# Attention, gated layer and softplus layer on one core: where 1/rms is applied for the first 1024 tokens of layer 1

## The chip, the core and the metric

The kernel runs on one core of one Trainium2 chip. The metric is the device time of one execution in microseconds; the time before is the median of three runs. All times below come from those runs and from one profiled execution.

## What is computed

```python
# q, k, v: (4, 8, 576, 64); x: 2304 tokens x 512
scores = scale * np.matmul(q, k.transpose(0, 1, 3, 2))
scores = np.where(masks[None], scores, -1e9)        # 4 heads local, 4 heads strided
attn = softmax(scores)                              # + 1e-9 in the divisor
x = np.matmul(attn, v) -> (2304, 512)

rms = np.sqrt(np.mean(x * x, axis=-1, keepdims=True) + 1e-06)
xn = x / rms * rms_g
g = xn @ w_gate                                     # 512 x 1536
silu = g * (1.0 / (1.0 + np.exp(-g)))
y = silu * (xn @ w_val) @ w_out                     # 1536 x 512

h = y @ w_in                                        # 512 x 2048
out = (np.maximum(h, 0.0) + np.log1p(np.exp(-np.abs(h)))) @ w_out2
```

Attention over 4 batches of 576 tokens with 8 heads gives x, 2304 tokens of 512 features. Layer 1 divides each token by its root mean square, multiplies by a gain for each feature, and forms silu(gate) * value through 1536 hidden features. Layer 2 is a softplus layer through 2048 hidden features. The division by rms is one number for each token, so it commutes with the products over features: a gate or a value made of undivided x is the true one times rms.

## The kernel before, in words

**Layout.** Features lie on the 128 partitions, tokens along the free dimension. x (the tile xs) is four blocks of 128 features (kk = 0 to 3). The tokens are cut into chunks of 512 (CUTS): chunks 0 and 1 are side A (tokens 0 to 1023), chunks 2, 3 and 4 (256 tokens) side B. The hidden features of layer 1 are 12 blocks of 128, called f in the code and hidden blocks here.

**Products.** Each fp32 operand is split in two rounded parts: ScalarE copies it to the rounded type (L351 for x, L405 and L425 for weights) and VectorE or GpSimd subtracts (L355 on VectorE, L356 on GpSimd). A product is three matmuls (mm3, L434): high by high, high by low, low by high. On side A each gate or value of a chunk is 12 matmuls into one bank (plain). On side B, and in layer 2, a product of 2 x 2 blocks is done with seven instead of eight block products (quad), from sums of chunks that combine builds and sums of weights.

**Attention and its place.** The first 16 of 32 attention units (two batches) run by themselves, with the weights of hidden blocks 0 and 1 decoded beside them. Chunk 0 is complete before these units end: at step 12 the function early works out its statistics, normalizes it, splits it and starts its first gate and value. The other 16 units are dealt out beside hidden blocks 0 to 9 of side A.

**Statistics.** stats (L440) squares the four blocks of x on ScalarE (L452), sums them over partitions and blocks with matmuls by a matrix of -1/512 (L453), takes logarithm and exponential on ScalarE (L457, L458), does one correction step in three VectorE instructions (L459, L461, L462) and leaves 1/rms in the tile ssq. norm (L467) then scales x in place: one fused VectorE instruction for each of the four blocks (L472), which multiplies by the gain and by 1/rms.

```python
def early():                       # L999, chunk 0; chunk 1 has the same three steps at L1071
    use.s = s_banks
    stats(0, f_banks)
    direct(0)                      # split_op of the four blocks of x
    half(0, 0, f_banks)            # gate and value of hidden block 0
```

**Gate chain.** chain1 (L860) reads a gate out of its bank with SiLU on ScalarE (L867) into a work tile of the ring gv, multiplies by the value out of its bank on VectorE (L868), and splits the result (L856 and L355) for the output product. out1 (L885) adds output products into x's own place (L899 for the first, L901 for all others).

**Work tiles.** The ring gv has two tiles of its own. Once chunks 0 and 1 are normalized, their 1/rms is of no more use, and the two halves of ssq join the ring (L1078), which then has four. From then on gates, statistics, the temporaries of combine and the copies of quad (L816) take turns on the four.

**Order.** The instructions are first noted in Program, each with an engine, a duration estimate and what it reads and writes. emit (L89) plays them through a model of the engines (Trial), eight times with due times that follow from the last play, and issues the best play's order, which then stands for every engine, queues of SyncE and GpSimd included. Two programs are emitted: up to hidden block 9 of side A with all of attention, and all that follows. An element-wise instruction added with two (L354) may be put on VectorE or on GpSimd.

Of the kernel before, what the change touches and what calls it, by code (L numbers as in the profile page):

```python
# [10 lines left out]
F32 = mybir.dt.float32  # L11
# [17 lines left out]
CH = 512  # L29
# [7 lines left out]
W1N, W2N = DFF // 128, DF2 // 128  # L37
DEALT = 10
LT, LT2, LV, EB = 4, 4, 5, 5
WARM = 9  # L40
# [207 lines left out]
def attn_glu_softplus(  # L248
# [99 lines left out]
    def split_op(src, ksrc, slot, k, n0=0, eng="POOL"):  # L348
# [3 lines left out]
        sub(eng, n, l, src, h.bitcast(F32), [ksrc, kh], [kl])  # L352

    def two(eng, n, name, o, x, y, r, w):  # L354
        pr.add("DVE", 68 + n / 0.96, lambda: getattr(nc.vector, name)(o, x, y), r, w,  # L355
               alt=(110 + n * 2.3, lambda: getattr(nc.gpsimd, name)(o, x, y)))  # L356
# [3 lines left out]

    hold = []

    def decode(src, t, kt, keep):

        raw, kraw = raws.next()
        u, ku = cvu.next()
        words = raw.bitcast(U32).rearrange("p (n two) -> p n two", two=2)
        wlo, whi = words[:, :, 0], words[:, :, 1]
        dma(512, lambda: nc.sync.dma_start(out=raw, in_=src), hold, [kraw])
        act(512, lambda: nc.scalar.activation(t, whi.bitcast(F32), AF.Copy, scale=2.0 ** -112), [kraw], [kt])  # L370
        dve(512, lambda: nc.vector.tensor_scalar(out=u, in0=t.bitcast(U32), scalar1=0x80000000, scalar2=None,
                                                 op0=ALU.bitwise_and), [kt], [ku], True)
        dve(512, lambda: nc.vector.scalar_tensor_tensor(  # L373
            out=u, in0=wlo, scalar=29, in1=u, op0=ALU.logical_shift_right, op1=ALU.bitwise_or),
            [kraw, ku], [ku])
        dve(512, lambda: nc.vector.scalar_tensor_tensor(
            out=t.bitcast(U32), in0=t.bitcast(U32), scalar=3, in1=u,
            op0=ALU.logical_shift_left, op1=ALU.bitwise_or), [kt, ku], [kt])
        dma(256, lambda: nc.sync.dma_start(out=wk[keep], in_=t), [kt], [("wk", keep, keep + 1)])

# [59 lines left out]
    def stats(c, ring_):  # L440
# [5 lines left out]
        for i, kk in enumerate((0, 2, 1, 3) if c < 2 else (0,)):  # L446
            y, ky = r, kr
            if c < 2:
# [14 lines left out]
                                                       op0=ALU.add, op1=ALU.mult), [kr, ks], [kr])  # L463
        if c < 2:
            norm(c, "DVE")
# [12 lines left out]
    def attention(at, use):  # L478
# [5 lines left out]
        mask = at.tile([128, MW], BF16, name="mask")  # L484
        dma(100, lambda: nc.sync.dma_start(out=mask, in_=masks), [], [all_of("mask")])
        vb = ring(at, "vb", 2, [128, 9, 128])
        eb = ring(at, "eb", EB, [128, 5 * LK])
        pp = ring(at, "pp", 2, [128, 6, 128])
        pt = ring(at, "pt", 4, [128, 3 * 128])
        sq = ring(at, "sq", 2, [128, 6 * SK])  # L490
        mz = ring(at, "mz", 8, [128, 2, 6])
# [29 lines left out]
        def load_v(u):  # L521
            b, p, t0, n = units[u]
            kp, nt = (LK, 9) if p < 2 else (128, 6)
            vt, (kv, _, _) = vb.next()
            src = vl[b, p] if p < 2 else vs[b, p - 2]
            vals[u // 2] = (vt, kv)
            dma(nt * (48 if p < 2 else 50), lambda: nc.sync.dma_start(out=vt[:kp, :nt, :], in_=src), [], [all_of(kv)])

# [118 lines left out]
        def stage_v(u):  # L647
# [8 lines left out]
            for a in range(n):  # L656
                t, kt = pts[a // 3]
                for h in range(2):
                    o = (2 * (a % 3) + (h ^ (u % 2))) * nq
                    pr.add("PE", 59, lambda a=a, h=h, o=o, t=t: nc.tensor.matmul(  # L660
                        xb[64 * h:64 * h + 64, a * nq:(a + 1) * nq], lhsT=vt[r0:r1, v0 + a, 64 * h:64 * h + 64],
                        rhs=t[r0:r1, o:o + nq], start=True, stop=True), [all_of(kv), kt],
                        [kx], mode=1 if loc else 3)
# [195 lines left out]

    def chain1(gate, val, n=CH, r4=False, eng="POOL"):  # L860
        (gb, kg), (vb_, kv) = gate, val
        if "bank" in kg[0]:
            a, ka = fk["gv"].next()
        else:
            a, ka = gb, kg
        a, gb, vb_ = a[:, :n], gb[:, :n], vb_[:, :n]
        act(n, lambda: nc.scalar.activation(a, gb, AF.Silu), [kg], [ka], True)  # L867
        dve(n, lambda: nc.vector.tensor_mul(a, vb_, a), [kv, ka], [ka])  # L868
        return halves(a, ka, n, eng, r4)
# [108 lines left out]
    with tc.manual_schedule():  # L978
# [9 lines left out]
        def direct(c):  # L988
            slots = (B11, B21) if c % 2 == 0 else (B12, B22)
            for kk in range(KD):  # L990
                x, kx = xview(kk, CUTS[c], CUTS[c + 1])
                split_op(x, kx, slots[kk // 2], kk % 2, eng="DVE" if kk % 2 or c and kk < 3 else "POOL")

        gates = {}

        def half(f, c, ring_):
            gates[f, c] = [plain(w_at(f, 0), row, c, ring_) for row in (0, 1)]

        def early():  # L999
            use.s = s_banks  # L1000
            stats(0, f_banks)
            direct(0)
            half(0, 0, f_banks)

        def prepare(f, parts, u):
# [13 lines left out]

        dma(64, lambda: nc.sync.dma_start(out=id_sb, in_=ident), [], [all_of("id")])  # L1020
        dma(2, lambda: nc.sync.dma_start(out=rg_sb, in_=rg), [], [all_of("rg")])
# [13 lines left out]
        def side_a(f, queue):  # L1035

            if f > 1 and f != DEALT:
                prep1(f, 0)
            w = w_at(f, 0)
            for c in (0, 1) if f > 1 else (1,):  # L1040
                gate, val = gates.pop((f, c), (None, None))
                gate = gate or plain(w, 0, c, f_banks)
                step(queue)
                drain(1)
                val = val or plain(w, 1, c, f_banks)
                step(queue)
                g[f, c] = chain1(gate, val, eng="DVE" if f < DEALT else "POOL")
                drain(1 if f < W1N - 1 else 0)
                step(queue)
            if f % 2:  # L1050
                todo.extend(outs1(f, f == 1, (0, 1) if f > 1 else (1,)))

        with ExitStack() as c2:
# [7 lines left out]
            for f in (0, 1):  # L1061
                g[f, 0] = chain1(*gates.pop((f, 0)))
            o_banks.t = f_banks.t
# [5 lines left out]
            o_banks.keys = {}  # L1069
            table(EXP_LN)  # L1070
            stats(1, t_banks)  # L1071
            table("silu_and_others")
            direct(1)
            half(0, 1, v_banks)
            tv = Ring(banks.t[2:4], "bank", 2)
            use.t = use.v = tv
            for i in (0, 1):
                fk["gv"].keys[len(fk["gv"].t)] = ("ssq", i * CH, i * CH + CH)  # L1078
                fk["gv"].t.append(ssq[:, i * CH:i * CH + CH])
# [5 lines left out]
            prep1(DEALT, 0)  # L1085
            pr.emit()
        o_banks.t = banks.t[4:6] + banks.t[2:4]
        o_banks.keys = {i: (f"bank{i}", 0, 1 << 20) for i in (2, 3)}
# [5 lines left out]
        for f in range(DEALT, W1N):  # L1094
            side_a(f, [None, None, (last_turn,)] if f == DEALT else [])
            if f == DEALT:
                combine(*SIDES[1][:2], False)
        drain(len(todo))
        o_banks.t, o_banks.keys = banks.t[4:], {}
        build(*SIDES[1], False)  # L1100
# [117 lines left out]
```

## Time and profile before

| | us |
|---|---|
| median of 3 runs | 901.63 |
| lowest, highest | 901.39, 902.55 |
| profiled execution | 900.52 |
| its span, first to last instruction | 898.7 |
| TensorE busy | 882.7 |
| VectorE busy | 712.9 |
| ScalarE busy | 486.1 |
| GpSimd busy | 28.1 |

PE is TensorE's matmul, PEld its weight load, DVE VectorE, ACT ScalarE, POOL GpSimd, SP SyncE. The span lies 1.8 us below its execution's time. Busy time of one engine says nothing by itself of who waits; for that there are the idle times with what ended them, and the chain of work that ended last. A line such as L355 is a helper's and serves many tiles, so groups are told apart by tiles: "ob<-xs,ob" writes the low part of x's operand, "win<-w,win" that of a weight.

### The profile page before, as it was taken

To read this page: it belongs to the slowest core of one execution; us is meant where nothing else is said; L and a number is where in the kernel's file an instruction comes from. 1 tells how busy PE (TensorE), PEld (TensorE's weight loads), DVE (VectorE), ACT (ScalarE), POOL (GpSimd) and SP (SyncE) were. 2 spreads that over 40 slices of the span, in tenths; PEclk is the share of its full clock that TensorE was granted. 3 is DMA by queue.
4 is the path that set the end of the run, shared out by engine and by line. 5 is a ranking of instruction groups with operands and counts; after the bars stand their busy time and mean duration, and the time that the engine had idled before them with its cause. 6 is when DMAs were issued, how large, how long until landed. Compare 5 with 4: busy or idle time off the path is not lost.

```text
span 898.7 us, 14075 instructions
## 1 busy us (share of the span) xinstructions
PE 882.7 (98%) x5320; PEld 725.7 (81%) x5320; DVE 712.9 (79%) x1349; ACT 486.1 (54%) x999; POOL 28.1 (3%) x26
## 2 busy tenths in 40 slices
PE   7899999999999999999999999999999999999998
PEld 6567777778777888888888888888888888888886
DVE  4988898998599995888988799877798456676644
ACT  5987664545364675444545567544474655434331
POOL 0000010200000000000100100000000000000000
PEclk7999999999999999999999999999999999999999
DMA  7874667363040443344553025321114111111003
GB/s 254 263 228 146 205 205 224 124 214 106 13 141 23 151 152 105 134 146 140 183 154 104 2 85 178 137 71 48 47 47 153 36 47 48 47 32 39 1 1 117
DMA packets 41858, 102.18 MB, mean 114 GB/s; under 512 B 4800, under 2 KB 5568, under 8 KB 41792
## 3 DMA queue, kind: packets, MB, share of 16 engines
q1 hardware_dynamic: 41792, 101.31, 35.5%
q8 instruction: 41, 0.67, 0.3%
q14 instruction: 25, 0.20, 0.1%
HBM read 78.74 MB, written 22.54 MB: 113 GB/s over the span
## 4 chain that ended last, share of the span: by engine, by line
PE 67%; DVE 3%; issue 0%
PE bank L434 67%; DVE xs L901 1%; DVE ob L355 0%; DVE tb L355 0%; DVE xs L355 0%; DVE win L355 0%; DVE w L355 0%; DVE ssq L355 0%; DVE glx L355 0%; DVE xs L919 0%; DVE gv L355 0%; DVE ssq L868 0%; DVE gv L868 0%; DVE gl L355 0%
## 5 line engine op out<-in xcount | busy, mean ns | idle before, releaser
L434 PE MATMUL bank<-ob,win 128*128 128x512 f32 (+1 forms) x1560 | 430.8, 360 | 2.7 <-ACT ob L351 1.8
L434 PEld LDWEIGHTS bank<-ob,win 128*128 128x128 f32 x1560 | 283.4, 188 | 55.0 <-ACT ob L351 2.2
L434 PE MATMUL bank<-tb,win 128*128 128x512 f32 x672 | 232.8, 392 | 0.0
L434 PEld LDWEIGHTS bank<-tb,win 128*128 128x128 f32 x672 | 125.4, 188 | 22.9 <-DVE xs L901 0.4
L919 DVE TENSOR_TENSOR xs<-bank,xs 128x512 f32<-128x512 f32 x126 | 86.8, 689 | 45.7 <-PE bank L434 44.4
L405 ACT ACTIVATE win<-w 128x512 fp32r<-128x512 f32 (+1 forms) x136 | 83.4, 616 | 63.9 <-PE bank L434 32.7
L355 DVE TENSOR_TENSOR win<-w,win 128x512 fp32r<-128x512 f32 (+1 forms) x134 | 89.5, 673 | 15.6 <-ACT win L405 12.6
L434 PE MATMUL bank<-wout,ghx 128*128 128x512 f32 x304 | 100.0, 390 | 0.0
L434 PE MATMUL bank<-wout,gh 128*128 128x512 f32 x272 | 90.4, 390 | 0.0
L434 PE MATMUL bank<-ghx,wout 128*128 128x512 f32 x224 | 84.1, 394 | 0.0
L434 PE MATMUL bank<-gh,wout 128*128 128x512 f32 (+1 forms) x256 | 81.3, 356 | 0.5 <-DVE xs L901 0.4
L901 DVE TENSOR_TENSOR xs<-bank,xs 128x512 f32<-128x512 f32 (+1 forms) x100 | 62.2, 628 | 8.9 <-PE bank L434 8.1
L434 PEld LDWEIGHTS bank<-wout,ghx 128*128 128x128 f32 x304 | 56.9, 188 | 11.7
L434 PEld LDWEIGHTS bank<-wout,gh 128*128 128x128 f32 x272 | 50.9, 188 | 10.6
L816 ACT ACTIVATE gv<-bank 128x512 f32<-128x512 f32 x48 | 28.4, 592 | 48.1 <-PE bank L434 47.6
L434 PE MATMUL bank<-wout,glx 128*128 128x512 f32 x152 | 53.2, 389 | 0.0
L434 PEld LDWEIGHTS bank<-gh,wout 128*128 128x128 f32 x256 | 45.5, 189 | 9.0 <-DVE xs L901 1.4
L434 PEld LDWEIGHTS bank<-ghx,wout 128*128 128x128 f32 x224 | 41.9, 188 | 8.4 <-ACT ghx L856 0.2
L434 PE MATMUL bank<-wout,gl 128*128 128x512 f32 x136 | 47.7, 389 | 0.0
L373 DVE SCALAR_TENSOR_TENSOR cvu<-raw,cvu 128x512 uint32<-128x512 uint32 x68 | 46.6, 686 | 1.0
L355 DVE TENSOR_TENSOR w<-w 128x256 f32<-128x256 f32 x109 | 45.4, 416 | 0.9
L820 DVE TENSOR_TENSOR gv<-bank,gv 128x512 f32<-128x512 f32 x48 | 32.9, 685 | 16.0 <-ACT gv L816 9.0
(131 smaller groups left out, 1211.8 us busy)
## 6 DMA issues: line engine op xcount, KB each, us to landing
raw<-w SPq DMA_DIRECT2D x68, 512.0 KB, 4.1
w<-w_kept SPq DMA_DIRECT2D x56, 256.0 KB, 2.6
w_kept<-cvtx SPq DMA_DIRECT2D x26, 256.0 KB, 3.7
cvt<-w_kept SPq DMA_DIRECT2D x26, 256.0 KB, 2.7
w_kept<-w SPq DMA_DIRECT2D x24, 256.0 KB, 4.2
qk<-qk SPq DMA_DIRECT2D x8, 601.0 KB, 5.6
w_kept<-cvt SPq DMA_DIRECT2D x18, 256.0 KB, 3.5
cvtx<-w_kept SPq DMA_DIRECT2D x18, 256.0 KB, 2.8
```

Source lines behind the costliest of these rows:

```text
L355: pr.add("DVE", 68 + n / 0.96, lambda: getattr(nc.vector, name)(o, x, y), r, w, alt=(110 + n * 2.3, lambda: getattr(nc.gpsimd, name)(o, x, ...
L373: dve(512, lambda: nc.vector.scalar_tensor_tensor(out=u, in0=wlo, scalar=29, in1=u, op0=ALU.logical_shift_right, op1=ALU.bitwise_or), [kra ...
L405: act(n, lambda: nc.scalar.activation(h, t, AF.Copy), [kt], [reg(0, o + lo, o + hi)])
L434: lambda a=a, b=b, i=i, st=st, mv=mv: nc.tensor.matmul(o, lhsT=st[a], rhs=mv[b], start=(first and i == 0), stop=(last and i == m - 1), ski ...
L816: act(CH, lambda: nc.scalar.activation(o, y[0], AF.Copy), [y[1]], [ko])
L820: dve(CH, lambda: nc.vector.tensor_add(o[0], y[0], o[0]), [y[1], o[1]], [o[1]])
L901: dve(n, lambda: nc.vector.tensor_add(x, pb, x), [kp, kx], [kx])
L919: dve(DM, lambda: nc.vector.tensor_add(x, pb, x), [kp, kx], [kx])
```

## The change

For chunks 0 and 1 x is not divided by rms ahead of layer 1. The operands are split from x times the gain alone (raw_op): a ScalarE copy with the gain as scale, and a fused VectorE instruction that multiplies and subtracts. The first gates and values of a chunk are noted ahead of its statistics. chain1 multiplies the gate by 1/rms on VectorE, out of the bank into the work tile, ahead of SiLU, which then works in place; the value stays undivided, and x is multiplied by 1/rms once after the last output product of side A (eight instructions that may go to VectorE or GpSimd). As ssq is needed until then, the ring gv gets two other tiles (gvx) while attention lives, goes back to two when the first program has been emitted, and gets the halves of ssq after the final multiplies. Some duration estimates in the planner change too: loads of weights, masks, values and of the identity (64 to 40), and the value products of the strided heads.

```diff
+RAW = (0, 1)
...
+    def raw_op(src, ksrc, slot, k, kk):
+        (h, l), (kh, kl) = op_of(slot, k)
+        g, kg = rg_sb[:, kk:kk + 1], all_of("rg")
+        act(CH, lambda: nc.scalar.activation(h, src, AF.Copy, scale=g), [ksrc, kg], [kh])
+        pr.add("DVE", 130 + CH / 0.96, lambda: nc.vector.scalar_tensor_tensor(
+            out=l, in0=src, scalar=g, in1=h.bitcast(F32), op0=ALU.mult, op1=ALU.subtract), [ksrc, kh, kg], [kl])
...
-        dma(512, lambda: nc.sync.dma_start(out=raw, in_=src), hold, [kraw])
+        dma(340, lambda: nc.sync.dma_start(out=raw, in_=src), hold, [kraw])
...
-        dma(256, lambda: nc.sync.dma_start(out=wk[keep], in_=t), [kt], [("wk", keep, keep + 1)])
+        dma(170, lambda: nc.sync.dma_start(out=wk[keep], in_=t), [kt], [("wk", keep, keep + 1)])
...
-        if c < 2:
+        if c < 2 and c not in RAW:
             norm(c, "DVE")
...
-        dma(100, lambda: nc.sync.dma_start(out=mask, in_=masks), [], [all_of("mask")])
+        dma(140, lambda: nc.sync.dma_start(out=mask, in_=masks), [], [all_of("mask")])
...
+        gvx.update((i, at.tile([128, CH], F32, name=f"gvx{i}")) for i in RAW)
...
-            dma(nt * (48 if p < 2 else 50), lambda: nc.sync.dma_start(out=vt[:kp, :nt, :], in_=src), [], [all_of(kv)])
+            dma(nt * (31 if p < 2 else 41), lambda: nc.sync.dma_start(out=vt[:kp, :nt, :], in_=src), [], [all_of(kv)])
...
-                    pr.add("PE", 59, lambda a=a, h=h, o=o, t=t: nc.tensor.matmul(
+                    pr.add("PE", 59 if loc else 36, lambda a=a, h=h, o=o, t=t: nc.tensor.matmul(
...
-    def chain1(gate, val, n=CH, r4=False, eng="POOL"):
+    def chain1(gate, val, n=CH, r4=False, eng="POOL", c=None):
...
+        if c in RAW:
+            r, kr = sview(CUTS[c], CUTS[c + 1]), ("ssq", CUTS[c], CUTS[c + 1])
+            dve(n, lambda a=a, gb=gb: nc.vector.tensor_mul(a, gb, r), [kg, kr], [ka])
+            gb, kg = a, ka
         act(n, lambda: nc.scalar.activation(a, gb, AF.Silu), [kg], [ka], True)
...
         def direct(c):
...
+                if c in RAW:
+                    raw_op(x, kx, slots[kk // 2], kk % 2, kk)
+                    continue
                 split_op(x, kx, slots[kk // 2], kk % 2, eng="DVE" if kk % 2 or c and kk < 3 else "POOL")
...
+        def give(cs):
+            for c in cs:
+                fk["gv"].keys[len(fk["gv"].t)] = ("ssq", c * CH, c * CH + CH)
+                fk["gv"].t.append(ssq[:, c * CH:c * CH + CH])
...
         def early():
             use.s = s_banks
-            stats(0, f_banks)
             direct(0)
             half(0, 0, f_banks)
+            stats(0, v_banks)
...
             table(EXP_LN)
+            direct(1)
+            half(0, 1, v_banks)
             stats(1, t_banks)
             table("silu_and_others")
-            direct(1)
-            half(0, 1, v_banks)
...
             for i in (0, 1):
+                if i in RAW:
+                    fk["gv"].keys[len(fk["gv"].t)] = (f"gvx{i}", 0, CH)
+                    fk["gv"].t.append(gvx[i])
+                    continue
                 fk["gv"].keys[len(fk["gv"].t)] = ("ssq", i * CH, i * CH + CH)
...
             pr.emit()
+            if RAW:
+                fk["gv"].t, fk["gv"].keys = fk["gv"].t[:2], {}
+                give(i for i in (0, 1) if i not in RAW)
...
         drain(len(todo))
+        for c in RAW:
+            for kk in range(KD):
+                x, kx = xv(kk, c)
+                two("POOL", CH, "tensor_mul", x, x, sview(CUTS[c], CUTS[c + 1]), [kx, ("ssq", CUTS[c], CUTS[c + 1])], [kx])
+        give(RAW)
```

## Rows read from the trace of the kernel before

**Rows 1.** The page: busy time, share and instructions of each engine.

```profile
PE 882.7 (98%) x5320; PEld 725.7 (81%) x5320; DVE 712.9 (79%) x1349; ACT 486.1 (54%) x999; POOL 28.1 (3%) x26
```

**Rows 2.** Windows: length, then busy us (x instructions) of PE, PEld, DVE, ACT, POOL; clock, DMA.

```profile
28.00:77.00 49.00, 42.95 (x478) 29.16 (x474) 41.91 (x100) 44.15 (x144) 0.00 (x0) 1.00 0.68 215
77.00:244.00 167.00, 166.60 (x1303) 131.89 (x1302) 144.15 (x292) 89.05 (x159) 13.35 (x10) 1.00 0.51 159
244.00:264.00 20.00, 19.98 (x87) 15.90 (x86) 19.47 (x33) 14.19 (x22) 1.41 (x1) 1.00 0.50 147
264.00:291.00 27.00, 26.25 (x114) 20.67 (x112) 27.00 (x49) 14.06 (x26) 1.29 (x1) 1.00 0.10 28
291.00:320.00 29.00, 29.00 (x153) 24.60 (x152) 28.12 (x56) 18.22 (x33) 1.30 (x1) 1.00 0.42 137
```

**Rows 3.** The chain that ended last: start us, us, what.

```profile
289.46 0.61 DVE xs L901
...
291.31 223.95 PE bank L434 x1172
```

**Rows 4.** TensorE's waits over the span: us in total, times, longest.

```profile
PE bank L434 <- ACT ob L351: 1.8, 2, 1.4
...
PE bank L453 <- ACT gv L452: 1.0, 2, 0.5
...
PE bank L637 <- DVE pp L355: 1.0, 1, 1.0
...
PE bank L434 <- DVE xs L901: 0.6, 2, 0.4
```

**Rows 5.** TensorE in order of time: start us, us, what, [idle before].

```profile
44.40 0.73 PE L434 MATMUL bank<-ob,win 128*128 128x512 f32 x2 [1.36 <-ACT ob L351]
...
76.55 8.02 PE L434 MATMUL bank<-ob,win 128*128 128x512 f32 x34 [0.39 <-ACT ob L351]
```

**Rows 6.** VectorE in order of time, the same columns.

```profile
42.72 2.07 DVE L472 SCALAR_TENSOR_TENSOR xs<-xs,rg_sb,ssq 128x512 f32<-128x512 f32 x3
...
257.32 2.38 DVE L355 TENSOR_TENSOR xs<-xs,ssq_b 128x512 f32<-128x512 f32 x2
...
278.30 0.68 DVE L355 TENSOR_TENSOR gv<-xs,ssq 128x512 f32<-128x512 f32 x1
...
279.83 0.67 DVE L355 TENSOR_TENSOR win<-w,win 128x512 fp32r<-128x512 f32 x1
...
280.43 0.68 DVE L901 TENSOR_TENSOR xs<-bank,xs 128x512 f32<-128x512 f32 x1
...
286.84 0.68 DVE L355 TENSOR_TENSOR tb<-gv,tb 128x512 fp32r<-128x512 f32 x1
...
289.38 1.87 DVE L901 TENSOR_TENSOR xs<-bank,xs 128x512 f32<-128x512 f32 x3
...
298.23 0.69 DVE L373 SCALAR_TENSOR_TENSOR cvu<-raw,cvu 128x512 uint32<-128x512 uint32 x1
```

**Rows 7.** Groups by line and shape: busy us, mean ns, idle before.

```profile
L472 DVE SCALAR_TENSOR_TENSOR xs<-xs,rg_sb,ssq 128x512 f32<-128x512 f32 x8 | 5.6, 745 | 0.0
...
L867 ACT ACTIVATE gv<-bank 128x512 f32<-128x512 f32 x13 | 7.8, 599 | 7.7 <-PE bank L434 6.4 <-DVE tb L355 1.2
...
L867 ACT ACTIVATE gv<-gv 128x512 f32<-128x512 f32 x12 | 7.6, 633 | 10.2 <-DVE gv L820 10.1
```

**Rows 8.** ScalarE in order of time.

```profile
58.58 0.28 ACT L281 ACTIVATE xs<-bank 128x128 f32<-128x128 f32 x1
...
58.91 0.37 ACT L281 ACTIVATE xs<-bank,rg_sb 128x128 f32<-128x128 f32 x1
...
276.13 0.58 ACT L867 ACTIVATE ssq<-bank 128x512 f32<-128x512 f32 x1
...
295.05 0.60 ACT L816 ACTIVATE gv<-bank 128x512 f32<-128x512 f32 x1 [4.48 <-PE bank L434]
```

**Rows 9.** GpSimd in order of time.

```profile
257.14 1.41 POOL L356 TENSOR_TENSOR xs<-xs,ssq_b 128x512 f32<-128x512 f32 x1 [48.80 <-DVE ssq_b L462]
```

## What the change is expected to do

> **What bounds the kernel now.** I read the page first: TensorE is busy 98% of the span, VectorE 79% [rows 1]. An average says little here, so next come windows cut where the work changes [rows 2]. TensorE is idle 6.05 us between 28 and 77 us (49.00 - 42.95), 0.4 us between 77 and 244, 0.75 between 264 and 291, and nothing from 291 to 320. From 77 us on TensorE is the bound, and what the change can win lies almost wholly ahead of 77. VectorE is the close second: full between 264 and 291 (27.00 of 27.00), nearly full from 244 to 320, but with 22.85 us to spare between 77 and 244. The chain that ended last says the same: it runs through VectorE up to 290 us, then through matmuls without a break [rows 3].
>
> TensorE's own waits [rows 4] tell what ends its idle time. Two kinds belong to this change: 1.8 us for the rounded operand of x (the copy of L351) and 1.0 us for squares (L452), in sum 2.8 us. TensorE's order of time says where [rows 5]: the first layer-1 products of chunk 0 start at 44.40 after 1.36 us of idleness, those of chunk 1 at 76.55 after 0.39. In between TensorE is not starved: scores, value products and the output products of the first two hidden blocks fill it.
>
> **Part by part.** One 512-wide VectorE instruction costs its engine 0.60 us: the addition out of a bank at 280.43 follows the subtraction at 279.83 by that much, and of three additions in 1.87 us the last is 0.68 long [rows 6]. The fused scaling of L472 costs 0.66: three in 2.07 [rows 6], one being 0.745 long [rows 7].
>
> [...]
>
> *Removed:* eight scalings of x (L472), 8 x 0.66 = 5.3 us of VectorE, four from 42.72 on, four around 76. With them goes the wait of the first products for the whole statistics chain: squares, sums, logarithm, exponential, three VectorE steps, scalings.
>
> *Added to the operands:* the copies of L351 get a per-partition scale, and the eight subtractions become fused ones at 0.66: 8 x 0.06 = 0.5 us more of VectorE, which the 5.3 us pay. The scaled copy has no row at this size; nothing at one end, 0.09 us each at the other, after the 128-wide pair at 58.58 and 58.91, 0.28 without and 0.37 with the scale [rows 8]. I take 0.09, 0.7 us in all; between 28 and 77 ScalarE has 4.85 us to spare [rows 2], and without that cover the 0.7 us would come on top.
>
> *Moved:* squares, sums and root of both chunks go behind the first gate and value products and use other banks; TensorE's work stays the same, so only idle time can be won. The 2.8 us of rows 4 go, since the rounded copies now need x alone; what is late next are chunk 0's weights (L405, L355). The other 3.25 us between 28 and 77 end on attention's exponentials, on weights and on probabilities such as those of L637 [rows 4]. They may stay (0) or go whole (3.25): on ScalarE four squares and two root steps no longer precede exponentials and weights, while four scaled copies do. No row is nearer to one end, so I take half, 1.6. The front gives **4.4 us**, with bounds 0 and 6.05.
>
> *Gate multiplies:* 24 at 0.60. Two (chunk 0, blocks 0 and 1) lie near 60 us, 18 between 77 and 244: 10.8 us into 22.85 us of slack. I cost them at nothing; without the cover TensorE would pay at most 10.8. They lengthen each chain by one step; a bank is wanted again only after a group of 12 matmuls, more than 2 us later, so this hides too. SiLU now reads SBUF, 633 against 599 ns [rows 7], nothing on an engine that is busy 89.05 of 167 us. The last four (blocks 10 and 11) fall between 244 and 291, where VectorE has 0.53 us left: 4 x 0.60 - 0.53 = **1.9 us**, charged in full, because TensorE there already waits for VectorE's additions [rows 3, 4].
>
> *Final multiplies:* eight, 4.8 us on VectorE or more on GpSimd, after the last additions of chunks 0 and 1 (three in 1.87 us from 289.38 on [rows 6]) and ahead of the next use of the two halves of ssq as work tiles. After 291 VectorE also decodes layer-2 weights (298.23 [rows 6]), which nothing needs soon and which can give way: I take 0 and keep 4.8 as the other end.
>
> *Work tiles:* from block 10 to the end of side A two instead of four serve the gate chains, the statistics and six temporaries of the sums for chunks 2 and 3. No row shows it. One end is 0. The other: the last gate chain took a tile at 276.13 [rows 8], and with two it would wait for the last temporary, written at 278.30 and read until 286.84 + 0.68 [rows 6], 11.4 us. I take 0: an unhurried temporary needs some 2.5 us (write, copy, subtract, hops), so six through two tiles some 7.5, and TensorE has output products to go on with.
>
> *Planner's estimates:* loads of weights, masks and values and the strided value product get other ones. They cost no time, but reorder every queue, SP's too. I take 0, and 1 us to both sides, the size of the single waits in rows 4.
>
> **Sum.** -4.4 + 1.9 = -2.5 us. The profiled execution took 900.52 (span 898.7 and 1.8 around it), so 898.0; the median of the runs is 1.1 above that execution, so 901.63 - 2.5 = **899.1 us**. About 0.2%, 1.8 us, is what a measurement can tell from no change.
>
> **Rivals.**
> *Nothing measurable (0.27).* The first products start earlier, but TensorE was filled anyway; only the 2.8 us go, and some 2.2 come back from VectorE: 901.0. It also covers a change that doesn't do what it says, because attention's ScalarE work holds x itself up. For it: the 3.25 us end on other things. Against it: ScalarE is relieved where it is nearly full.
>
> *The hand-over pays (0.18).* Between 244 and 300 VectorE has no room, and the ring of work tiles takes back the halves of ssq only after the eight multiplies. Those end at 289.38 + 1.87 + 4.8 = 296.0 if nothing goes between, while the first products of the next chunks were copied into work tiles from 295.05 on [rows 8]. It decides as soon as such a copy lands on a half of ssq before the multiplies are through; behind it a bank stays full and TensorE stands. Price: 12 x 0.60 = 7.2 us, with the front at 2.8: 901.63 + 4.4 = 906.0. For it: TensorE waits for L901 there already. Against it: chunk 0's four can run among chunk 1's additions.
>
> *The shared port (0.05).* While GpSimd multiplied x at 257.14, for 1.41 us [rows 9], VectorE's pair of the same operation took 2.38 us [rows 6] where two steps of 0.60 and 0.68 would have done. If GpSimd takes all eight beside such work, VectorE stands 8 x 1.41 = 11.3 us: 901.63 - 2.5 + 11.3 = 910.4. [...]
>
> *More than the waits (0.06).* All 6.05 us go, and the four multiplies hide: 895.6.
>
> **Numbers.** The forecast (a gain of 1.8 to 5 us) has 0.44. With the larger gain faster is 0.50; same is 0.27; the hand-over and the port make slower 0.23. The range runs from 895.0 (the whole front, with something of the planner's 1 us) to 906.0 (the hand-over); the likeliest case alone covers 896.6 to 899.8.
>
> **What would show it.** Right: the first product of rounded x with weights starts before 40 us, chunk 1's near 71; no L472 rows; TensorE's idle time between 28 and 77 under 3 us; a new VectorE group of 24 multiplies out of a bank; the products of the next chunks start some 2 us ahead of 291. Wrong: idle TensorE behind copies of L816 or behind the final multiplies after 290; a front as idle as now; waits for the multiplied gate in side A.

## The result and the profile after

The changed kernel took 912.38 us (median of four runs, 911.39 to 913.96) against 901.51 on the same chips (899.32 to 902.55): a ratio of 1.0136, interval 1.0113 to 1.016. It is 10.9 us slower; the forecast was 899.1, the range ended at 906.0. The profiled execution has a span of 911.4 us against 898.7.

The page's first part, of after: busy time, share of the span and instructions.

```profile
PE 884.3 (97%) x5320; PEld 727.0 (80%) x5320; DVE 723.6 (79%) x1365; ACT 485.1 (53%) x995; POOL 43.9 (5%) x38
```

Against [rows 1] TensorE's same 5320 matmuls are busy 1.6 us longer and the span is 12.7 longer: the other 11.1 us are TensorE's idle time. Windows of after, columns as in [rows 2], say where most of it lies:

```profile
28.00:77.00 49.00, 42.74 (x470) 31.91 (x468) 43.49 (x103) 39.95 (x134) 7.54 (x6) 0.97 0.72 221
77.00:244.00 167.00, 163.26 (x1216) 126.37 (x1215) 144.52 (x290) 87.94 (x153) 14.11 (x11) 0.99 0.49 152
244.00:264.00 20.00, 18.76 (x132) 14.80 (x133) 17.14 (x31) 14.20 (x23) 0.80 (x1) 1.00 0.45 129
264.00:291.00 27.00, 24.15 (x97) 18.89 (x97) 25.54 (x39) 12.69 (x22) 7.81 (x6) 0.94 0.07 23
291.00:320.00 29.00, 29.00 (x148) 24.61 (x147) 28.87 (x56) 15.18 (x30) 1.62 (x1) 1.00 0.15 46
```

The front, where the gain was to come from, is as idle as before: 6.26 us against 6.05. The stage that had no slack to lose, 77 to 244, is idle 3.74 us against 0.4, and from 244 to 291 4.09 against 0.77. These three make 6.9 us of the 11.1. The rest lies ahead of 28 us, 2.5, and behind 320, 1.8; the first of the two says little, since orders as fast as before (e3 and e8 below) are idle 1.3 and 2.5 us more than before there, too. VectorE's busy share isn't full ahead of 291, but from 258 to 283 us the chain that ended last runs through it with no pause over 1.02 us: there it is the bound.

The chain that ended last, of after (start us, us, what):

```profile
282.38 0.61 DVE gv L878
283.04 55.37 PE bank L442 x269
...
346.84 4.88 DMA w_kept<-cvtx
...
451.45 5.53 DMA w<-w_kept
```

A gate multiply (L878) is now a link of it, the last before 55 us of matmuls. And where [rows 3] show 223.95 us of matmuls without a break, transfers of weights stand in between.

TensorE's waits over the span, of after:

```profile
PE bank L562 <- ACT eb L608: 5.8, 2, 5.1
PE bank L646 <- DVE eb L363: 2.3, 2, 1.4
PE bank L442 <- DVE gv L878: 2.2, 3, 1.3
PE bank L646 <- DVE mz L595: 2.1, 1, 2.1
```

Of [rows 4] the waits for the rounded copies of x and for squares are gone but for 0.3 us (L460, not shown), as forecast. In their place stand attention's own waits and the new multiply's. TensorE in order of time, of after, against [rows 5]:

```profile
33.39 2.68 PE L442 MATMUL bank<-ob,win 128*128 128x512 f32 x10
...
47.99 0.72 PE L646 MATMUL bank<-id_sb,eb 128*96 128x128 f32 x5 [2.13 <-DVE mz L595]
...
50.27 0.30 PE L562 MATMUL bank<-mask 64*64 64x270 bf16 x2 [0.72 <-ACT eb L608]
...
52.52 0.31 PE L646 MATMUL bank<-id_sb,eb 128*96 128x128 f32 x1 [1.37 <-DVE eb L363]
```

Chunk 0's products do start 11 us earlier. Where they stood before, from 44.40 to some 53, attention's exponentials and sums now have nothing beside them, and TensorE stands 4.2 us in three pieces.

The groups by line and shape, of after, answer to [rows 7]; the last two are the fused subtraction and the scaled copy:

```profile
L880 ACT ACTIVATE gv<-gv 128x512 f32<-128x512 f32 x28 | 17.6, 629 | 20.9 <-DVE gv L878 14.9 <-DVE gv L829 5.8
L878 DVE TENSOR_TENSOR gv<-bank,ssq 128x512 f32<-128x512 f32 x16 | 10.9, 685 | 2.0 <-PE bank L442 1.7
L878 DVE TENSOR_TENSOR gvx<-bank,ssq 128x512 f32<-128x512 f32 x8 | 5.5, 685 | 3.2 <-PE bank L442 3.2
L359 DVE SCALAR_TENSOR_TENSOR ob<-xs,rg_sb,ob 128x512 fp32r<-128x512 f32 x8 | 5.9, 749 | 0.0
L358 ACT ACTIVATE ob<-xs,rg_sb 128x512 fp32r<-128x512 f32 x8 | 5.9, 743 | 0.0
```

The L472 rows are gone and 24 multiplies of 0.685 us are there. SiLU used to wait for matmuls, 6.4 us in the group of [rows 7]; now it waits 14.9 us for the multiply.

### The profile page after: what moved, and what is told of

It reads as the page before. It is cut to its first block, busy times and chain, and to the rows that moved or that the text cites. A ratio compares the mean times of both kernels' runs of the same rounds, so it can differ in the third digit from the quotient of the medians.

```text
span 911.4 us, 14103 instructions
## 1 busy us (share of the span) xinstructions
PE 884.3 (97%) x5320; PEld 727.0 (80%) x5320; DVE 723.6 (79%) x1365; ACT 485.1 (53%) x995; POOL 43.9 (5%) x38
## 4 chain that ended last, share of the span: by engine, by line
PE 79%; DVE 9%; DMA 6%; ACT 4%; issue 1%; SPq 0%; ACTq 0%; DVEq 0%
PE bank L442 75%; DMA raw<-w 2%; DMA w_kept<-cvtx 2%; PE bank L669 1%; PE bank L646 1%; DMA qk<-qk 1%; DVE xs L914 1%; PE bank L575 1%; ACT eb L608 1%; DVE cvu L381 1%; DVE win L363 1%; DMA w<-w_kept 1%; DVE gl L363 1%; DVE gv L363 1%; DVE tb L363 1%
## 5 line engine op out<-in xcount | busy, mean ns | idle before, releaser
L442 PE MATMUL bank<-ob,win 128*128 128x512 f32 (+1 forms) x1560 | 439.5, 365 | 3.6 <-DVE gv L878 2.2
L363 DVE TENSOR_TENSOR win<-w,win 128x512 fp32r<-128x512 f32 (+1 forms) x127 | 84.3, 668 | 16.2 <-ACT win L413 13.1
```

Source lines behind the costliest of these rows:

```text
L442: lambda a=a, b=b, i=i, st=st, mv=mv: nc.tensor.matmul(o, lhsT=st[a], rhs=mv[b], start=(first and i == 0), stop=(last and i == m - 1), ski ...
```

## The experiments

The change has two parts that need not go together: x undivided with 1/rms moved behind, and new duration estimates in the planner. I had costed the second at 0 plus or minus 1 us. The theories at the start: the new estimates make a worse order (A); the moved 1/rms costs by itself (B), and there by VectorE's time for the multiplies, by the smaller ring of work tiles, by the final multiplies, or by something else; or any other order of the same instructions gains or loses this much (C). "Before" in each result was measured on the same chip; all times are medians.

**Each part alone.** e1_est_only is before with all six estimates, e2_raw_only the change with the old ones.

```diff
-        dma(512, lambda: nc.sync.dma_start(out=raw, in_=src), hold, [kraw])
+        dma(340, lambda: nc.sync.dma_start(out=raw, in_=src), hold, [kraw])
...
-                    pr.add("PE", 59, lambda a=a, h=h, o=o, t=t: nc.tensor.matmul(
+                    pr.add("PE", 59 if loc else 36, lambda a=a, h=h, o=o, t=t: nc.tensor.matmul(
```

> The kernel before with the change's six duration estimates and nothing else of it. Theory A (the estimates): the planner now believes loads land sooner and issues weight loads ahead of attention's own, so the loss of 11 us is here: 908 to 914 us, TensorE idle some 7 us before 28 us as with the whole change. Theory B (the multiplies and tiles of the moved 1/rms): the estimates alone leave the time within 2 us of before, 899 to 904, whatever the first 28 us look like. Theory C (order luck, any other plan costs or gains some us): anything between 897 and 912, with no part of the loss tied to the loads.

> The whole change with the duration estimates of before. Theory A: the loss goes, 896 to 902 us, and the front gain of some 4 us that the prediction named is seen. Theory B: 909 to 914, with idle TensorE behind the gate multiplies between 77 and 244 us and at the hand-over near 283. Theory C: anything between 897 and 912.

Measured: e1 909.21 (ratio 1.0096, 1.0066 to 1.0126), e2 907.78 (1.0082, 1.0055 to 1.0108). Both cost, 8.5 and 7 us, and together 10.9: they don't add up. e2 lies under the range given for B and far over the one for A.

**How much is the order that happened to be drawn?** emit weighs each play's due times against those of the one before with KEEP = 0.5; another value gives other orders of the same program. e3 is before, e4 the change, both with 0.4; e15 is e1, e16 is e2 with 0.6.

```diff
-TURNS, KEEP, SWITCH, LEAVE = 8, 0.5, 125, 4000
+TURNS, KEEP, SWITCH, LEAVE = 8, 0.4, 125, 4000
```

> The kernel before with one planner constant moved that no instruction knows of (how much of the last play's due times is kept: 0.4 for 0.5). It measures how far another plan for the same instructions moves the time. Theories A and B: within 2 us of before, 899.5 to 903.5. Theory C: off by 4 us or more.

> The changed kernel with the same planner constant at 0.4. Theories A and B: still slower than before by 8 us or more, 909 to 915. Theory C: it falls back by 4 us or more, to 908 or less.

> The six estimates alone, with the planner's constant at 0.6 for another order. If the estimates themselves are the cause (orders made for faster loads and value products lose whatever their detail): 906 to 911 us. If the order found was a poor draw: 904 or less.

> The moved 1/rms with the estimates of before and the constant at 0.6. If the edit is the cause: 905 to 910 us. If a poor draw: 904 or less.

Measured: e3 901.21 (1.0006, 0.9993 to 1.0019), e4 910.25 (1.0115, 1.0081 to 1.0148), e15 905.99 (1.0054, 1.0039 to 1.007), e16 908.8 (1.0073, 1.005 to 1.0096). The loss isn't one unlucky draw, as far as two orders of each can tell. The moved 1/rms costs about the same in both; of the estimates' 8.5 us some 3 are the draw's, and e15 lies between its two forecasts.

**Which estimates?** e7 is before with the two for weights (340 and 170), e8 before with the other four.

> The kernel before with the two estimates for weights alone (loading a weight 340 for 512, keeping it 170 for 256). If the loss of the estimates comes from weight loads put ahead of attention's loads: 905 to 911 us, TensorE idle 7 us or more before 28 us. If it comes from the others: 899 to 903.

> The kernel before with the other four estimates alone (mask, identity, values, strided value product). If weight loads are the cause: 899 to 903 us. If the estimate of the value product or of the values is: 905 to 911.

Measured: e7 903.93 (1.0041, 1.0022 to 1.0061), e8 900.5 (1.0005, 0.9992 to 1.0018). The weights' estimates cost by themselves, less than was said for them; the other four cost nothing alone, and whether they add to the weights' isn't shown: e15, all six in another order, has 1.0054, inside e7's interval. Idle TensorE ahead of 28 us, which was to mark the cause, marks nothing: e8 has 7.4 us of it and is as fast as before.

The chain that ended last of e7 passes through transfers:

```profile
311.63 5.61 DMA w<-w_kept
318.32 0.65 ACT cvtx L370
319.50 70.69 PE bank L434 x374
...
539.36 6.58 DMA raw<-w
```

In [rows 3] there is none. Of these two, raw<-w is a load with a new estimate; w<-w_kept has kept its own and reads back a decoded weight. Over all 68 loads raw<-w the time from issue to decode step has a median of 8.6 us in before, 8.0 in e7, 7.5 in e1 and 6.9 in after, worked out from the traces: a load believed shorter is issued somewhat later, though other kernels with the old estimates lie as low as 7.8 (e5). What parts the two kinds is ScalarE's idle time that ends with a transfer's landing: in sum 15.9 us in before and 12 to 23 in the others with the old weights' estimates, but 40.9 in e7, 52.8 in e1, 33.2 in e15 and 42.3 in after. ScalarE of after shows such a wait in side A, in order of time:

```profile
114.32 0.68 ACT L378 ACTIVATE w<-raw 128x512 f32<-128x512 f32 x1 [2.00 <-DMA raw<-w]
114.90 0.62 ACT L880 ACTIVATE gv<-gv 128x512 f32<-128x512 f32 x1
...
115.68 0.46 ACT L282 ACTIVATE xs<-bank,rg_sb 128x256 f32<-128x256 f32 x1
```

SiLU starts at 114.90, though its multiply had ended at 113.92 (113.24 and 0.68, in VectorE's rows below): it and attention's copy stand behind a decode step that waited 2.00 us for its weights. TensorE, in its own order of time, waits for a gate multiply and then for that copy:

```profile
113.98 0.97 PE L442 MATMUL bank<-ob,win 128*128 128x512 f32 x3 [0.49 <-DVE gv L878]
116.20 0.90 PE L646 MATMUL bank<-id_sb,pp 128*128 128x128 f32 x3 [1.25 <-ACT xs L282]
```

**The ring of two tiles and the final multiplies.** e9 is before with two work tiles between the programs and the end of side A. e10 is e2 without the eight final multiplies; its x stays undivided after side A.

```diff
+            kept, fk["gv"].t = fk["gv"].t[2:], fk["gv"].t[:2]
...
         drain(len(todo))
+        fk["gv"].t += kept
```

> The kernel before with one thing taken away: between the two emitted programs and the end of side A the ring of work tiles has two tiles, as in the change, and not four; the halves of ssq join again ahead of side B. If the short ring is what the hand-over pays for: 903 to 907 us, with TensorE idle between 264 and 300 us where before it was idle 0.75. If a temporary can simply be asked for earlier, as the prediction had it: 899 to 902.

> The change with the duration estimates of before and without the eight final multiplications of x by 1/rms, which are left out; the halves of ssq join the ring at the same place. If the eight are a cost: some 3 us under the same kernel with them, 903 to 905. If decoding gives way to them, as the prediction had it: 906 to 909.

Measured: e9 901.09 against 901.08 (1.0001, 0.9989 to 1.0012), e10 908.74 (1.0095, 1.0078 to 1.0112). Neither is the cause by itself.

**The gate multiplies.** e5 is before with 24 multiplies by 1.0 between bank and SiLU; e6 is e2 without its own, so that the gates stay undivided.

```diff
+        if n == CH and "bank" in kg[0]:
+            dve(n, lambda a=a, gb=gb: nc.vector.tensor_scalar(out=a, in0=gb, scalar1=1.0, scalar2=None, op0=ALU.mult),
+                [kg], [ka])
+            gb, kg = a, ka
         act(n, lambda: nc.scalar.activation(a, gb, AF.Silu), [kg], [ka], True)
```

> The kernel before, with one thing added: each of the 24 gates of side A is multiplied by 1.0 out of its bank on VectorE ahead of SiLU, as the change multiplies it by 1/rms. If the extra VectorE step in the gate chain is what the moved 1/rms costs: 905 to 909 us, idle TensorE behind that step between 77 and 244 us. If VectorE's slack there covers it, as the prediction had it: 899 to 903.

> The change with the duration estimates of before, and without the multiplication of the gate by 1/rms; SiLU is taken of the undivided gate, so the 24 multiplies are left out and nothing else. If they are the cost: back to 898 to 902 us, or below before where the earlier start of the first products pays. If the reordering of the first 80 us is the cost: still 905 to 909.

Measured: e5 902.86 (1.0032, 1.0017 to 1.0047), e6 901.88 (1.0024, 1.0013 to 1.0035). Each kernel is taken against before on its own chip, whose medians differ by up to 1.5 us: e2 loses 7.0 us and e6 2.3, so the multiplies are some 4.8 us of e2's loss, and 3.3 in before. e5 lies in the range given for slack that covers the step (899 to 903), but its interval excludes no change. And the early start, alone in e6, gains nothing.

**One chunk at a time.** e11 changes chunk 0 only, e12 chunk 1 only, both with the old estimates.

```diff
-RAW = (0, 1)
+RAW = (0,)
```

> The change for chunk 0 alone, with the duration estimates of before; chunk 1 is normalized as before, and its half of ssq joins the ring. Half of the multiplies, a ring of three tiles at the hand-over, four final multiplies. If the costs are those of the multiplies and the ring: half of the loss, 902 to 906 us. If starting chunk 0's products early itself strands TensorE later in the attention units (it was idle around 50 us in all kernels that did it): as slow as with both chunks, 905 to 909.

> The change for chunk 1 alone, with the duration estimates of before. Costs of multiplies and ring: 902 to 906 us. If chunk 0's early start is the cost: 899 to 902, and below before if the 0.8 us of chunk 1's waits go and the cover holds.

Measured: e11 905.7 (1.0054, 1.0038 to 1.0069), e12 905.5 (1.0048, 1.0029 to 1.0067). Each chunk costs over half of the 7 us, so the cause isn't chunk 0's start inside attention alone.

**Time or step?** e13 is e2 with the multiply on 32 of 512 columns: SiLU still comes after it and reads the bank (most of the gate stays undivided). e14 is e2 without gate multiplies, with 20 reductions of 512 columns on VectorE, tied to nothing.

```diff
-            dve(n, lambda a=a, gb=gb: nc.vector.tensor_mul(a, gb, r), [kg, kr], [ka])
-            gb, kg = a, ka
+            dve(32, lambda a=a, gb=gb: nc.vector.tensor_mul(a[:, :32], gb[:, :32], r[:, :32]), [kg, kr], [ka])
```

> The change with the duration estimates of before, the gate multiplied in 32 of its 512 columns only; SiLU reads the bank as before and still waits for that short step, so the rest of the multiplication is left out. If the added step in the chain (two hand-overs between engines) is the cost: 906 to 908 us, as with the full multiply. If VectorE's time of 24 x 0.60 us is: near the kernel without the multiplies, 901 to 903.

> The change with the duration estimates of before, without the gate multiplies (left out), and with 20 VectorE instructions of the same length (a maximum over 512 columns of the mask) in hidden blocks 0 to 9 that nothing waits for. If VectorE's time is the cost wherever it stands: 905 to 908 us. If it is free unless tied to a gate, since VectorE has slack: 901 to 903.

Measured: e13 908.46 (1.0082, 1.0067 to 1.0097), e14 902.13 (1.0011, 1.0 to 1.0022). Most of the multiplies' VectorE time, without the tie: nothing (20 of 24; the four of hidden blocks 10 and 11, where VectorE is fullest, have no untied counterpart). The tie with little of the time: the full price.

**Step or 1/rms?** In e13 every first gate also waits for its chunk's 1/rms. e17 is e2 with multiplies by 1.0, so that no gate waits for it; e18 is before with a multiply by 1.0 on 32 columns ahead of SiLU.

```diff
+        if n == CH and "bank" in kg[0]:
+            dve(32, lambda a=a, gb=gb: nc.vector.tensor_scalar(out=a[:, :32], in0=gb[:, :32], scalar1=1.0, scalar2=None,
+                                                              op0=ALU.mult), [kg], [ka])
```

> The change with the estimates of before, and with each gate multiplied by 1.0 over its 512 columns instead of by 1/rms (the division by rms of the gates is left out): the 24 extra steps stay in the chains at their full length, but no gate waits for the statistics of its chunk. If the extra step itself is what the gate multiplies cost, it stays near 907.8, the value with 1/rms (907 to 909). If instead the first gates' banks being held until 1/rms is there is the cost, it comes near the kernel without gate multiplies, 901.9, or, with the price of 24 untroubled steps in before (3.3 us), near 904 to 905.

> Before, with each gate of layer 1 of the first 1024 tokens multiplied by 1.0 on VectorE on 32 of its 512 columns, and SiLU still reading the bank but only after this step: the chain gets one more step and one more hand-over, VectorE next to no work. The full multiplies gave 902.9 against 899.6. If the step and its hand-overs are what costs, it is near that again, 902 to 904; if VectorE's time is, 900 to 901.5.

Measured: e17 906.29 (1.0083, 1.0055 to 1.0111), e18 902.8 (1.0034, 1.0019 to 1.0048). The step is most of the cost, and not what it waits for: e17's interval is nearly e2's, and in e5 and e18 1/rms plays no part. By medians e17 is 5.9 us over its before and e2 7.0, between the two forecasts, so a price of some 1 us for waiting for 1/rms isn't excluded. The step's width doesn't matter: in before 0.34% with 32 columns, 0.32% with 512.

Where the step costs shows in TensorE's idle time between 77 and 244 us. It is 0.4 us in before and 0.7 to 1.3 in the other kernels without a step that have the old weights' estimates (e3, e6, e8, e9, e14). With the step it is 2.0 and 2.3 in e18 and e5, and 2.3 to 4.1 in all seven that move 1/rms with the old estimates (e2, e10 to e13, e16, e17), two orders of e2 among them. The windows of e2, then e6, columns as in [rows 2]:

```profile
77.00:244.00 167.00, 163.30 (x1250) 126.29 (x1250) 150.56 (x298) 90.68 (x157) 16.00 (x13) 1.00 0.51 160
```

```profile
77.00:244.00 167.00, 165.74 (x1291) 128.98 (x1289) 140.22 (x285) 89.78 (x157) 10.83 (x10) 1.00 0.51 159
```

TensorE's waits between 77 and 291 us show what the step does. First e18, then e2, then e14, which has no step; before has here, of [rows 4], the 0.6 us for L901, one wait of 0.4 for L351 and one of 0.2 of attention.

```profile
PE bank L434 <- ACT ssq L870: 1.2, 1, 1.2
PE bank L434 <- DVE xs L904: 0.9, 2, 0.7
PE bank L434 <- ACT gv L870: 0.5, 1, 0.5
```

```profile
PE bank L442 <- DVE gv L878: 1.5, 3, 0.8
PE bank L646 <- DVE xs L280: 1.0, 2, 0.7
PE bank L442 <- DVE gvx L881: 1.0, 1, 1.0
```

```profile
PE bank L442 <- DVE gv L467: 0.5, 1, 0.5
PE bank L647 <- DVE xs L280: 0.5, 2, 0.3
```

L870 of e18 is SiLU, L878 and L881 of e2 are the two multiplies of the chain. With the step TensorE waits for the chain to empty a bank, 1.7 us in e18 and 2.9 in e2 (1.5, 1.0 and one of 0.4 not shown); without it, never (L467 belongs to the statistics). VectorE of after, in order of time, shows how an instruction of 0.6 us can do that:

```profile
112.63 0.69 DVE L381 SCALAR_TENSOR_TENSOR cvu<-raw,cvu 128x512 uint32<-128x512 uint32 x1
113.24 0.68 DVE L878 TENSOR_TENSOR gv<-bank,ssq 128x512 f32<-128x512 f32 x1
113.84 0.68 DVE L384 SCALAR_TENSOR_TENSOR w<-w,cvu 128x512 uint32<-128x512 uint32 x1
```

In the order that emit chose, the multiply stands among the steps that decode weights, and SiLU on ScalarE behind such a step (114.32 above). In the change the gate's bank is free after a place on VectorE instead of one on ScalarE, and the value's bank after three places (multiply, SiLU, multiply) instead of two; in e13 and e18, where SiLU still reads the bank, the gate's too is free after two instead of one. Is it the places, or the way from engine to engine? VectorE's step and ScalarE of e18, in order of time:

```profile
161.12 0.18 DVE L868 TENSOR_SCALAR gv<-bank 128x32 f32<-128x32 f32 x1
161.33 0.60 ACT L870 ACTIVATE gv<-bank 128x512 f32<-128x512 f32 x1 [1.19 <-DVE gv L868]
...
256.51 0.18 DVE L868 TENSOR_SCALAR ssq<-bank 128x32 f32<-128x32 f32 x1
257.64 0.63 ACT L405 ACTIVATE win<-w 128x512 fp32r<-128x512 f32 x1
258.18 0.58 ACT L870 ACTIVATE ssq<-bank 128x512 f32<-128x512 f32 x1
```

The first SiLU starts 0.03 us after its step has ended, the second 1.5 us, behind other work of ScalarE. In 14 of e18's 24 gates it is under 0.1 us, in nine over 0.4, worked out from the trace. So the way itself is short, and it is the places that are long.

**Where each part is lost.** The first product of the next chunks (tb by win) divides the run: its start, and what is left of the span behind it, in one profiled execution of each.

```
                          start    span    rest
before                   291.31   898.7   607.4
after                    300.98   911.4   610.4
e2  1/rms moved          299.99   907.5   607.5
e13 the same, 32 columns 298.98   906.9   607.9
e17 the same, by 1.0     295.29   903.9   608.6
e6  no gate multiplies   292.02   899.8   607.8
e14 untied work          291.38   899.1   607.7
e5  step in before       291.99   899.9   607.9
e18 short step in before 293.17   900.8   607.6
e1  all estimates        297.34   907.0   609.7
e7  weights' estimates   291.51   903.1   611.6
e15 e1, another order    294.01   902.9   608.9
```

The moved 1/rms loses nearly everything ahead of that product; behind it e2 and e13 lose 0.1 and 0.5 us, e17 1.2. The weights' estimates lose 1.5 to 4.2 us behind it, and with the other four up to 6 ahead of it. After is the sum of both kinds: 9.7 us ahead, 3.0 behind.

No version beat before.

## Why the prediction was wrong

**The planner's estimates: "I take 0, and 1 us to both sides".** This step failed by 5 to 8.5 us: 8.5 in e1, 5 in another order, 4 from the weights alone. The text said that estimates reorder every queue and then priced that by the size of a single wait. In before the chain runs 224 us through matmuls alone [rows 3] and no load is a link of it; with the new estimates the decode steps wait for transfers 33 to 53 us in sum instead of 12 to 23, and transfers are links.

**The gate multiplies: "They lengthen each chain by one step; a bank is wanted again only after a group of 12 matmuls, more than 2 us later, so this hides too".** I counted VectorE's time against its slack, and that half was right: 20 untied instructions cost nothing (e14). The step was the other half, and it measured 4.8 us with the early start and 3.3 and 2.4 without (e5, e18). What I left out is that on both engines of the chain a step takes a place among other work, in the order that emit chose, so that it adds this place and not its 0.6 us: in e18 one SiLU starts 0.03 us after its step has ended, another 1.5. That the last four alone would pay, 1.9 us, was wrong as to place: in e2, which has the old estimates, 77 to 244 lost 3.3 us and 244 to 291 0.5, as [rows 2] had slack on VectorE between 77 and 244 but none on TensorE.

**The front: "4.4 us".** The waits of [rows 4] went, the products started before 40 us, and nothing was won: e6 is 2.3 us slower than before. The text itself said that TensorE isn't starved between 44 and 77 because these products fill it. Moving them ahead took the filling away, and attention's waits, the other 3.25 us of which I hoped to win half, grew. That was the rival "nothing measurable", and I gave it too little: idle time that other work covers isn't won by moving the cover.

**Right, or of no weight.** The fused subtraction (749 against 684 ns for the plain one of after, 0.065 us; 0.06 taken) and the scaled copy (743 against 623, 0.12; 0.09 taken) hide but for little: in the trace of after no engine waits for either, and in e6 TensorE waits 0.3 us for the copy. Two work tiles cost nothing (e9), the final multiplies neither (e10): "the hand-over pays", whose 906.0 closed the range, is not what happened: in after TensorE is full from 291 to 320 us (29.00 of 29.00). In after the last gate multiply stands at 288.71 against a last chain at 276.13 [rows 8], but this lateness comes with the estimates and the step, and e9 shows that the ring alone doesn't make it.

**VectorE beside GpSimd**, the rival called the shared port, has a part that no run separates, and what the two engines share isn't shown. GpSimd rose from 28.1 to 43.9 us busy, though not by the final multiplies, all of which went to VectorE. GpSimd, then VectorE of after, in order of time:

```profile
264.58 1.83 POOL L364 TENSOR_TENSOR wout<-cvtx,wout 128x512 fp32r<-128x512 f32 x1
```

```profile
265.18 1.78 DVE L363 TENSOR_TENSOR gv<-xs 128x512 f32<-128x512 f32 x1
```

VectorE's instruction took 1.1 us more than the usual 0.68, and it ended 0.55 us after the one on GpSimd. Not every instruction beside GpSimd is longer: VectorE's addition out of a bank at 263.98 took 0.68. The rival's 11.3 us let VectorE stand for the whole of eight instructions on GpSimd, 1.41 us each; no run shows this term, and its own rows show 1.1 us beside the one of 1.41 (2.38 for the pair, against 0.60 and 0.68). Worked out from the traces, VectorE's instructions beside one on GpSimd took in sum 5.9 us more in after than the median of their kind, 5.4 in before; from 244 to 300 us, where the chain runs through VectorE, 3.9 against 1.9. In e2 the sum is 9.0, in e6 2.1, so a part of what the step costs behind an early start may come from there. It isn't all of it: in e5 and e18 the sum is 4.7 and 5.9, about as in before, and e11 loses 4.6 us with 3.3.

**Open.** Whether the same step, some 3 us in before, costs more behind an early start, as the medians say (3.6 in e17, 4.8 in e2 and 5.2 in e13, over e6, each against its own before), though the intervals overlap; why estimates and 1/rms together cost 4.7 us less than the sum of both; and whether the four small estimates do harm beside the weights'. A part of each is the order drawn: against its own before, a change of KEEP moved e1 by some 3.4 us and the change itself by 1.4, and e5, e6, e13, e14, e17 and e18 were measured in one order each. Whether a longer chain would hide with more banks for the gates isn't shown; none were added.

## What to carry to other kernels

A step added between a bank and its release can cost its places in the queues it passes rather than its duration (here 2.4 us with 32 columns, e18, and 3.3 with 512, e5): count who is in front of it on each engine, and test it with a version of almost no width. Work that TensorE does while it would wait for something else is cover (with it moved ahead, 28 to 77 us of e6 is idle 5.98 us against 6.05); before moving it earlier, say what will stand in its place. Duration estimates of a planner are part of the kernel: change them alone, and measure them alone.

## What the runs showed of the hardware

TensorE's granted clock fell in mid-kernel, which before shows at no place between 24 us and its last matmul. Windows of after, columns as in [rows 2], the clock third from the right:

```profile
47.60:51.00 3.40, 2.29 (x71) 2.04 (x71) 3.40 (x12) 3.05 (x18) 0.00 (x0) 1.00 0.90 282
51.00:54.40 3.40, 1.80 (x13) 1.25 (x10) 3.40 (x12) 3.27 (x13) 0.00 (x0) 0.96 0.95 321
54.40:57.80 3.40, 3.40 (x34) 2.46 (x34) 1.71 (x4) 1.69 (x11) 0.00 (x0) 0.54 0.79 289
57.80:61.20 3.40, 3.40 (x31) 2.64 (x25) 3.10 (x10) 2.89 (x6) 0.97 (x1) 1.00 0.57 158
```

TensorE was busy 2.29 and then 1.80 of 3.40 us; behind that the grant is 0.54, in stretches of 0.4 us 0.50 from 54.40 to 57.20 and full again from 57.60 on. After has such stretches near 118 and 284 us, too (0.99 and 0.94 in the windows above). In e6 TensorE was busy 1.77 of 3.40 us from 47.60 on and 1.81 from 51.00; the grant is 0.58 in the second of these and 0.50 in the full window behind. It isn't the early start's alone: e5, whose products start at 42.41, has 0.80 from 40.80 on with TensorE busy 1.79, and 0.70 in the full window behind.

So in these three runs the full stretch behind a sparse one had a grant of 0.54, 0.50 and 0.70. Not every sparse stretch is followed by that: in e8 TensorE was busy 1.21 and 2.56 of 3.40 us from 34.00 on, and the grant is 1.00 there and in the windows behind. The front of e6 as a whole reads:

```profile
28.00:77.00 49.00, 43.02 (x459) 32.40 (x459) 38.91 (x92) 40.53 (x134) 1.79 (x1) 0.93 0.67 213
```

It is idle 5.98 us, as long as before, at a mean grant of 0.93 against 1.00. Worked out from that row, 0.07 of 49 us is 3.4 us of TensorE at full clock that e6 lacks there. Whether this is why it ends 2 us behind before isn't shown: e14 has the same 0.93 there, is idle 4.69 us, and starts its next chunks' products at 291.38, as before does. Nor does the clock part the kernels with the step from those without: over the whole span the mean grant is 0.990 in e2 and 0.991 in e6 and e14. What share of the change's 10.9 us it has, no run separates.
